# Linear attention, MLP and Sinkhorn mixture of experts on one core: VectorE's queue taken from the scheduler, and eight weight conversions placed at other steps

## The chip, the cores and the metric

One core of a Trainium2 chip. The metric is the time of one run of the program in device microseconds (us); lower is better. The engines are named as in the profile: PE (TensorE, PEld its weight loads), DVE (VectorE), ACT (ScalarE), POOL (GpSimd) and SP (SyncE, which issues the transfers). Each engine works through its own queue, one instruction after the other, in an order fixed when the program is built; waits between engines go through semaphores.

## What is computed

The reference, cut to what matters:

```python
# attention: q, k, v are 4 x 8 x 576 x 64
q_s = softmax(q, axis=-1); k_s = softmax(k, axis=2)
kv  = einsum('bhsd,bhse->bhde', k_s, v)
x   = einsum('bhsd,bhde->bhse', q_s, kv)      # -> 2304 tokens x 512
# MLP: w_in 512 x 2048, w_out 2048 x 512
h = x @ w_in
x = maximum(0.01 * h, h) @ w_out
# experts: 8, each w1 512 x 1024, w2 1024 x 512
P = exp(x @ w_gate - max)
for _ in range(8):                            # Sinkhorn
    P /= P.sum(1) + 1e-9; P /= P.sum(0) + 1e-9; P *= N / E
out = sum over e of P[:, e] * (relu(x @ w1[e]) @ w2[e])
```

Matrix products are made of three matmuls each: both operands are held as a high and a low part, and high x high, high x low and low x high are added up in PSUM.

## The kernel before, in words

The program has three stages that overlap on the engines.

**Attention.** `k_task` (line 251) takes the exponential of one pair of heads of k: DVE finds the maximum (`knm`, L255), ACT the exponential with its sum (L257), PE transposes (`pk`, L265), ACT copies to `ke` (L267), PE multiplies with v (`pkv`), ACT scales into `kv` (L281). `q_task` (line 283) does the softmax of 128 tokens of q in place in `acc`: DVE maximum (`qmx`, L291), POOL subtraction (L293), ACT exponential (L295), DVE sum and reciprocal (`qsm`, L297 to L299), POOL product (L300), PE transpose (`pq`, L305), ACT copy back (L306). `x_task` (line 308) multiplies both (`px`) for one block of 384 tokens and splits the result into its high part (ACT, L331) and low part (DVE, L332) in `xs`. There are six blocks.

**MLP.** 96 steps: four phases of four 128-wide weight units over six blocks. A step `s` has two half-steps: in half-step 2s, `first` makes the hidden group `ph` (12 matmuls) of step s+1 (before step 14) or s+2, and ACT and DVE turn it into `hh` (L205 to L207); in half-step 2s+1, `second` multiplies `hh` of step s into four output groups `y0` to `y3` (12 matmuls). At a block's last unit the four groups are copied to `acc` by ACT (L226, in the first phase) or added to it by DVE (L228); the next block's `y` groups use the same four PSUM banks. The weights of the MLP arrive as 64-bit floats, and `prep_half` (line 138) converts half a unit over four half-steps: ACT absolute value (`ca`, L146); one half-step later three DVE ops (L148, L149, L152); one later the ACT cast of the high part (L156) and two DVE ops (L157, L158); one later a subtraction and an addition (L162, L163), on DVE for the first four units and on POOL for the others, and then the load of another half unit. Three raw buffers hold the loads.

**Experts.** 48 groups `group(i)` (line 571), each of seven parts with Strassen-like sums, and output tiles `e`. Gate and Sinkhorn (`balance`) run at its beginning.

What sets the order: up to the experts all code runs inside `tc.manual_schedule()` (line 74, closed at line 772 by `front.close()`), where each engine's queue is the order in which the source calls its instructions. The half-steps are a hand-written plan: `at(t, task)` starts a task in half-step t, and each `yield` of the task hands over to the next half-step. Behind line 772 the scheduler orders every queue by its own rules.

Of the kernel before, what the change touches and what calls it, by code (L numbers as in the profile page):

```python
# [22 lines left out]
def kernel(  # L23
# [47 lines left out]


    front = ExitStack()
    front.enter_context(tc.manual_schedule())
    const = ctx.enter_context(tc.tile_pool(name="const", bufs=1))
    hp_ = ctx.enter_context(tc.tile_pool(name="h", bufs=2))
    sk_p = ctx.enter_context(tc.tile_pool(name="sk", bufs=2))
# [45 lines left out]
    halves = ((0, 0), (1, 0), (0, 1), (2, 0), (1, 1), (3, 0), (2, 1), (3, 1))  # L123
# [526 lines left out]
    def at(t, f, *a):  # L650
        plan.setdefault(t, []).append((f, a))
# [74 lines left out]
    at(26, open_units)  # L726
    H2 = 2 * SP

    for t, (f, half) in zip((26, 28, 29, 32, 34, 36, 40, 42), halves):
        at(t, prep_half, PU + f, half)  # L730
    for ph in range(1, NPH - 1):
        for n, (f, half) in enumerate(halves):
# [40 lines left out]
    t = END  # L773
# [47 lines left out]
```

## Time and profile before

| | |
|---|---|
| median of 3 runs | 2020.96 us (2019.91 to 2023.77) |
| the profiled execution | 2021.46 us, its span 2019.6 us |
| busy in the span | PE 1990.9 us, PEld 1825.1, DVE 1300.8, ACT 806.7, POOL 486.5 |
| instructions | 26345 |
| moved by transfers | 138.56 MB, 68 GB/s from and to memory over the span |

The span is cut at times from its start. In a timeline row the first number is the start, the second the time from the first start to the last end of the merged instructions, xN their count, and the bracket the engine's idle time before it with what ended that. A wait belongs to the engine that idles. PEclk is the granted TensorE clock as a share of full speed.

### The profile page before, as it was taken

What the parts mean: (1) busy time and instruction counts of PE and PEld (TensorE: products, weight loads), DVE (VectorE), ACT (ScalarE), POOL (GpSimd) and SP (SyncE); (2) the same over time, 40 slices, a digit from 0 to 9 for tenths busy, and PEclk for the clock granted to TensorE, in tenths of its full rate; (3) what the DMA queues carried; (4) which work ended last, traced back from release to release, by engine and by line L of the source; (5) the groups of instructions that cost most, each with busy time, mean ns of one, the idle gap of its engine ahead of it and who ended that gap; (6) DMA issues with size and microseconds to landing.
All of it is one profiled execution on the core that took longest, in us unless ns stands there. A gap on an engine that the chain in (4) does not pass through costs nothing.

```text
span 2019.6 us, 26345 instructions
## 1 busy us (share of the span) xinstructions
PE 1990.9 (99%) x10323; PEld 1825.1 (90%) x10323; DVE 1300.8 (64%) x1953; ACT 806.7 (40%) x1367; POOL 486.5 (24%) x476
## 2 busy tenths in 40 slices
PE   7999999999999999999999999999999999999998
PEld 6999999999889999989999999999999999999997
DVE  7766435445786666666766666666686666666663
ACT  6654323234443333333444333334344333333331
POOL 3124222300223223122122231231322322313220
PEclk7999999999999999999999999999999999999999
DMA  6502111100212212212132122121212221211210
GB/s 221 175 12 81 45 43 42 53 1 1 85 43 84 84 42 84 70 56 84 42 115 84 43 84 73 54 84 48 78 68 89 84 82 44 84 55 72 84 42 32
DMA packets 65453, 138.56 MB, mean 69 GB/s; under 512 B 4656, under 2 KB 4656, under 8 KB 65328
## 3 DMA queue, kind: packets, MB, share of 16 engines
q1 hardware_dynamic: 65328, 136.87, 19.6%
q8 instruction: 81, 1.33, 0.3%
q14 instruction: 44, 0.36, 0.1%
HBM read 132.14 MB, written 4.72 MB: 68 GB/s over the span
## 4 chain that ended last, share of the span: by engine, by line
PE 73%; DVE 1%; ACT 0%; issue 0%; ACTq 0%; DVEq 0%
PE e L189 38%; PE pa L189 10%; PE pc L189 10%; PE pd L189 10%; PE pb L189 5%; DVE wa L458 0%; PE y L189 0%; DVE xs L565 0%; ACT wa L457 0%; DVE pm L399 0%; DVE cs L400 0%; PE pcs L189 0%; PE pt L189 0%; PE pg L189 0%; DVE rs L398 0%; DVE rs L396 0%
## 5 line engine op out<-in xcount | busy, mean ns | idle before, releaser
L189 PE MATMUL e<-wb_t,xs 128*128 128x512 f32 x3456 | 803.4, 390 | 0.0
L189 PEld LDWEIGHTS e<-wb_t,xs 128*128 128x128 f32 x3456 | 647.0, 188 | 131.2
L464 POOL TENSOR_TENSOR s<-pair 128x256 f32<-128x256 f32 x96 | 72.5, 755 | 1186.1 <-DMA pair<-in_w 719.3
L558 DVE SCALAR_TENSOR_TENSOR acc<-e,pm,acc 128x512 f32<-128x512 f32 x264 | 193.0, 743 | 99.5 <-PE e L189 98.3
L189 PE MATMUL pa<-xs,wa 128*128 128x384 f32 x1152 | 234.2, 337 | 0.0
L565 DVE SCALAR_TENSOR_TENSOR xs<-c,xs 128x384 fp32r<-128x384 f32 (+1 forms) x192 | 185.2, 983 | 70.9 <-ACT xs L564 70.9
L189 PE MATMUL pc<-xs,wa 128*128 128x384 f32 x1152 | 230.8, 334 | 0.0
L189 PE MATMUL pd<-xs,wa 128*128 128x384 f32 x1152 | 230.6, 334 | 0.0
L564 ACT ACTIVATE xs<-c 128x768 fp32r<-128x768 f32 x192 | 126.8, 682 | 231.8 <-PE e L189 211.1
L189 PEld LDWEIGHTS pa<-xs,wa 128*128 128x128 f32 x1152 | 204.6, 188 | 7.2
L189 PEld LDWEIGHTS pc<-xs,wa 128*128 128x128 f32 x1152 | 202.4, 188 | 0.2 <-issue 0.2
L189 PEld LDWEIGHTS pd<-xs,wa 128*128 128x128 f32 x1152 | 202.4, 188 | 0.1
L207 DVE TENSOR_TENSOR hh<-g,hh 128x384 fp32r<-128x384 f32 x96 | 58.4, 609 | 197.8 <-ACT g L206 197.8
L458 DVE TENSOR_TENSOR wa<-s,wa 128x768 fp32r<-128x768 f32 x96 | 91.8, 957 | 106.1 <-ACT wa L457 106.0
L457 ACT CAST wa<-s 128x768 fp32r<-128x768 f32 x96 | 80.2, 836 | 170.8 <-POOL s L467 150.2
L580 DVE TENSOR_TENSOR c<-c 128x384 f32<-128x384 f32 x96 | 53.9, 561 | 133.4 <-ACT c L600 133.4
L590 ACT COPY c<-pa 128x384 f32<-128x384 f32 x96 | 46.1, 480 | 198.9 <-PE pa L189 193.5
L458 DVE TENSOR_TENSOR wa<-pair,wa 128x1024 fp32r<-128x1024 f32 x96 | 120.2, 1252 | 5.2 <-ACT wa L457 5.1
L205 ACT ACTIVATE hh<-ph 128x384 fp32r<-128x384 f32 x96 | 47.3, 492 | 184.1 <-PE y L189 170.6
L458 DVE TENSOR_TENSOR wb_t<-pair,wb_t 128x1024 fp32r<-128x1024 f32 x96 | 114.1, 1223 | 7.0 <-PE y L189 3.2
L189 PE MATMUL y<-hh,wa 128*128 128x384 f32 x576 | 112.4, 344 | 4.2 <-ACT acc L226 3.6
L467 POOL TENSOR_TENSOR s<-pair,s 128x256 f32<-128x256 f32 x96 | 113.8, 1185 | 7.5
(117 smaller groups left out, 2528.7 us busy)
## 6 DMA issues: line engine op xcount, KB each, us to landing
pair<-in_w SPq DMA_DIRECT2D x192, 512.0 KB, 5.1
raw<-in_wm SPq DMA_DIRECT2D x32, 512.0 KB, 3.8
v<-in_vt SPq DMA_DIRECT2D x16, 320.0 KB, 5.8
k<-in_kt SPq DMA_DIRECT2D x16, 288.0 KB, 5.6
out<-acc SPq DMA_DIRECT2D x18, 256.0 KB, 2.0
acc<-in_q SPq DMA_DIRECT2D x5, 768.0 KB, 7.6
acc<-in_q SPq DMA_DIRECT2D x3, 256.0 KB, 6.3
wg_t<-in_wg SPq DMA_DIRECT2D x1, 16.0 KB, 3.5
```

What stands on the lines that cost most here:

```text
L189: nc.tensor.matmul(o, a, b, start=start, stop=stop, **more)
L205: nc.scalar.activation(hh[:, 0, :], p, AF.Prelu, alpha=0.01)
L207: nc.vector.tensor_tensor(hh[:, 1, :], g, r32(hh[:, 0, :]), op=ALU.subtract)
L457: nc.scalar.copy(hi, a)
L458: return lambda: nc.vector.tensor_tensor(lo, a, r32(hi), op=ALU.subtract)
L464: nc.gpsimd.tensor_tensor(s[:, 0], a21, a22, op=ALU.add)
L467: nc.gpsimd.tensor_tensor(s[:, 2], a12, s[:, 1], op=ALU.subtract)
L558: nc.vector.scalar_tensor_tensor(a, y, scale, a, op0=ALU.mult, op1=ALU.add)
L564: nc.scalar.activation(o[:, 0], p, AF.Relu)
L565: nc.vector.scalar_tensor_tensor(o[:, 1], p, 0.0, r32(o[:, 0]), op0=ALU.max, op1=ALU.subtract)
L580: add = lambda o, x, y: nc.vector.tensor_tensor(o, x, y, op=ALU.add)
L590: nc.scalar.copy(c1, bk[0])
```

## The change

```diff
     front = ExitStack()
-    front.enter_context(tc.manual_schedule())
+    E_ = mybir.EngineType
+    front.enter_context(
+        tc.manual_schedule(engines={E_.PE, E_.Activation, E_.Pool, E_.SP})
+    )
...
-    for t, (f, half) in zip((26, 28, 29, 32, 34, 36, 40, 42), halves):
+    for t, (f, half) in zip((26, 28, 32, 34, 36, 41, 43, 45), halves):
         at(t, prep_half, PU + f, half)
```

The first part takes DVE out of the manual order: up to the experts its queue is now what the scheduler makes of it, while PE, ACT, POOL and SP keep the order of the source. The second gives six of the eight conversions of the second phase's units other half-steps: none is left one half-step behind another, and the last one begins at 45 instead of 42.

The instructions are the same ones, 1953 on DVE in both programs. The queues of PE, POOL and SP hold them in the same order as before. On ACT the conversions between `hh16` and `hh25` have moved, and two casts of the second pair of expert weights stand three instructions earlier, ahead of `hh87`. On DVE most of the queue up to the experts is rearranged. Three places follow; the line numbers of the change are three higher, the number behind a name's last underscore is the buffer's, and `ca4_1` is unit 4, half 1.

**DVE in the startup**, behind the first conversion; `knm1_0` is the maximum of the first heads of k of batch 1, `qmx` and `qsm` belong to tiles of q, `ksm` to sums of k. Before:

```order
L163 TENSOR_TENSOR wa_84<-ca0_0_156,raw0_0_123 128x512
L255 TENSOR_REDUCE knm1_0_225<-k1_0_158 128x1
L291 TENSOR_REDUCE qmx2_228<-acc0_77 128x8
L268 TENSOR_SCALAR ksm0_2_166<-ksm0_2_166 128x1
L269 RECIPROCAL ksm0_2_166<-ksm0_2_166 128x1
L291 TENSOR_REDUCE qmx3_258<-acc1_78 128x8
L268 TENSOR_SCALAR ksm0_3_186<-ksm0_3_186 128x1
L269 RECIPROCAL ksm0_3_186<-ksm0_3_186 128x1
L297 TENSOR_REDUCE qsm1_189<-acc0_77 128x8
```

In the change:

```order
L166 TENSOR_TENSOR wa_84<-ca0_0_156,raw0_0_123 128x512
L294 TENSOR_REDUCE qmx2_228<-acc0_77 128x8
L271 TENSOR_SCALAR ksm0_2_166<-ksm0_2_166 128x1
L271 TENSOR_SCALAR ksm0_3_186<-ksm0_3_186 128x1
L272 RECIPROCAL ksm0_2_166<-ksm0_2_166 128x1
L272 RECIPROCAL ksm0_3_186<-ksm0_3_186 128x1
L300 TENSOR_REDUCE qsm1_189<-acc0_77 128x8
L301 TENSOR_SCALAR qsm1_189<-qsm1_189 128x8
L302 RECIPROCAL qsm1_189<-qsm1_189 128x8
L294 TENSOR_REDUCE qmx3_258<-acc1_78 128x8
L294 TENSOR_REDUCE qmx4_300<-acc1_78 128x8
L258 TENSOR_REDUCE knm1_0_225<-k1_0_158 128x1
```

`knm1_0` stood right behind the conversion's last op; it now stands behind the sum of q tile 1 (`qsm1`, which reads what ACT's exponential writes) and two more maxima.

**ACT at steps 15 to 17**, where block 3's output is copied to `acc3`. Before:

```order
L205 ACTIVATE hh16_1605<-ph16_1592 128x384
L206 ACTIVATE g16_1606<-ph16_1592 128x384
L146 ACTIVATE ca4_1_1617<-raw4_1_1114 128x512
L156 CAST wb_t_1533<-ca5_0_1572 128x512
L205 ACTIVATE hh17_1650<-ph17_1637 128x384
L206 ACTIVATE g17_1651<-ph17_1637 128x384
L156 CAST wb_t_1533<-ca4_1_1617 128x512
L226 COPY acc3_80<-y0_12_1505 128x384
L226 COPY acc3_80<-y1_12_1506 128x384
L226 COPY acc3_80<-y2_12_1507 128x384
L226 COPY acc3_80<-y3_12_1508 128x384
```

In the change:

```order
L208 ACTIVATE hh16_1605<-ph16_1592 128x384
L209 ACTIVATE g16_1606<-ph16_1592 128x384
L159 CAST wb_t_1533<-ca5_0_1572 128x512
L208 ACTIVATE hh17_1645<-ph17_1632 128x384
L209 ACTIVATE g17_1646<-ph17_1632 128x384
L229 COPY acc3_80<-y0_12_1505 128x384
L229 COPY acc3_80<-y1_12_1506 128x384
L229 COPY acc3_80<-y2_12_1507 128x384
L229 COPY acc3_80<-y3_12_1508 128x384
L149 ACTIVATE ca4_1_1670<-raw4_1_1114 128x512
```

The cast of unit 4's second half stood between `g17` and the four copies; it now comes behind them, after its absolute value.

**DVE at the end of a block in the last phase**: the additions into `acc2`, the split of a summed block (L458, `xs<-acc1`) and `hh85`. Before:

```order
L458 TENSOR_TENSOR xs_83<-acc1_78,xs_83 128x768
L458 TENSOR_TENSOR xs_83<-t1_0_4059,xs_83 128x768
L207 TENSOR_TENSOR hh85_4160<-g85_4161,hh85_4160 128x384
L458 TENSOR_TENSOR xs_83<-acc1_78,xs_83 128x768
L228 TENSOR_TENSOR acc2_79<-y0_80_4043,acc2_79 128x384
L228 TENSOR_TENSOR acc2_79<-y1_80_4044,acc2_79 128x384
L228 TENSOR_TENSOR acc2_79<-y2_80_4045,acc2_79 128x384
L228 TENSOR_TENSOR acc2_79<-y3_80_4046,acc2_79 128x384
L357 TENSOR_TENSOR xs_83<-acc2_79,xs_83 128x768
L207 TENSOR_TENSOR hh86_4198<-g86_4199,hh86_4198 128x384
```

In the change:

```order
L461 TENSOR_TENSOR xs_83<-acc1_78,xs_83 128x768
L461 TENSOR_TENSOR xs_83<-t1_0_4059,xs_83 128x768
L231 TENSOR_TENSOR acc2_79<-y0_80_4043,acc2_79 128x384
L231 TENSOR_TENSOR acc2_79<-y1_80_4044,acc2_79 128x384
L231 TENSOR_TENSOR acc2_79<-y2_80_4045,acc2_79 128x384
L231 TENSOR_TENSOR acc2_79<-y3_80_4046,acc2_79 128x384
L210 TENSOR_TENSOR hh85_4160<-g85_4161,hh85_4160 128x384
L461 TENSOR_TENSOR xs_83<-acc1_78,xs_83 128x768
L360 TENSOR_TENSOR xs_83<-acc2_79,xs_83 128x768
L493 TENSOR_TENSOR acc1_78<-acc1_78,t1_0_4059 128x768
L210 TENSOR_TENSOR hh86_4198<-g86_4199,hh86_4198 128x384
```

The four additions, which free the `y` banks, stood behind `hh85` and a split that waits for ACT; they now stand ahead of both.

## Rows read from the trace of the kernel before

**Rows 1.** The page, busy time of each engine (share of the span, instructions).
```profile
PE 1990.9 (99%) x10323; PEld 1825.1 (90%) x10323; DVE 1300.8 (64%) x1953; ACT 806.7 (40%) x1367; POOL 486.5 (24%) x476
```

**Rows 2.** Stretches: start:end, length, busy PE, PEld, DVE, ACT, POOL, PEclk, DMA share, GB/s.
```profile
0.00:48.65 48.65, 37.33 (x172) 30.45 (x173) 37.59 (x77) 30.79 (x71) 19.26 (x23) 0.72 0.62 217
60.00:67.30 7.30, 5.42 (x25) 5.39 (x26) 5.37 (x9) 3.65 (x8) 0.81 (x1) 0.77 0.33 103
...
570.00:2019.00 1449.00, 1444.57 (x7257) 1308.11 (x7255) 967.68 (x1317) 562.14 (x853) 346.32 (x360) 1.00 0.20 69
```

**Rows 3.** Waits of PE by its line and the releaser: us, times, longest.
```profile
PE pk L265 <- ACT k L257: 6.4, 3, 3.3
PE y L189 <- ACT acc L226: 3.6, 2, 2.6
...
PE ph L189 <- DVE xs L332: 1.9, 1, 1.9
PE y L189 <- DVE acc L228: 1.7, 2, 1.2
...
PE ph L189 <- ACT ke L267: 1.0, 1, 1.0
```

**Rows 4.** DVE in the startup: a stretch, and two lines' durations (ns min/median/max) there.
```profile
20.00:42.26 22.26, 17.91 (x65) 13.63 (x65) 21.54 (x45) 15.73 (x38) 11.06 (x10) 0.54 0.42 147
L149 DVE TENSOR_SCALAR ca<-ca x4: 1146/1147/1149, 9.4 to 55.3; 128x512 uint32<-128x512 uint32 x4
L158 DVE SCALAR_TENSOR_TENSOR raw<-raw x4: 692/1411/1415, 12.6 to 59.9; 128x512 f32<-128x512 uint32 x4
```

**Rows 5.** Timeline, startup: where its splits and the first hidden groups stand.
```profile
18.74 0.63 ACT L295 ACTIVATE acc<-acc 128x512 f32<-128x512 f32 x1 [1.97 <-POOL acc L293]
19.26 0.75 DVE L255 TENSOR_REDUCE knm<-k 128x1 f32<-128x576 f32 x1 [1.45 <-DMA k<-in_kt]
21.62 0.67 DVE L297 TENSOR_REDUCE qsm<-acc 128x8 f32<-128x512 f32 x1
42.26 1.00 DVE L332 TENSOR_TENSOR xs<-px,xs 128x384 fp32r<-128x384 f32 x2
48.65 4.41 PE L189 MATMUL ph<-xs,wa 128*128 128x384 f32 x24
```

**Rows 6.** Timeline, block 1's splits, and what PE does before and behind its wait.
```profile
61.28 1.01 DVE L332 TENSOR_TENSOR xs<-px,xs 128x384 fp32r<-128x384 f32 x2
61.88 1.18 PE L189 MATMUL ph<-xs,wa 128*128 128x384 f32 x5 [1.88 <-DVE xs L332]
64.41 3.19 PE L189 MATMUL y<-hh,wa 128*128 128x384 f32 x12
66.45 0.43 DVE L149 TENSOR_SCALAR ca<-ca 128x512 uint32<-128x512 uint32 x1
...
77.21 2.36 PE L189 MATMUL y<-hh,wa 128*128 128x384 f32 x12
```

**Rows 7.** Timeline, conversions of the second phase: ACT's cast and copies, PE behind them.
```profile
161.78 1.53 DVE L148 TENSOR_SCALAR ca<-ca 128x512 f32<-128x512 f32 x1
165.50 0.62 ACT L156 CAST wb_t<-ca 128x512 fp32r<-128x512 f32 x1 [2.75 <-DVE ca L152]
166.03 1.62 ACT L226 COPY acc<-y 128x384 f32<-128x384 f32 x4
166.55 2.39 PE L189 MATMUL y<-hh,wa 128*128 128x384 f32 x12 [2.62 <-ACT acc L226]
184.64 2.38 PE L189 MATMUL y<-hh,wa 128*128 128x384 f32 x12 [1.01 <-ACT acc L226]
```

**Rows 8.** Timeline, last phase: the additions of two blocks and PE behind them.
```profile
463.36 1.94 DVE L228 TENSOR_TENSOR acc<-y,acc 128x384 f32<-128x384 f32 x4
464.05 2.35 PE L189 MATMUL y<-hh,wb_t 128*128 128x384 f32 x12 [1.15 <-DVE acc L228]
484.01 2.35 PE L189 MATMUL y<-hh,wb_t 128*128 128x384 f32 x12 [0.59 <-DVE acc L228]
```

## The prediction

> **What bounds the kernel now.** I read the busy times first: PE works 1990.9 of 2019.6 us [rows 1], so the whole program runs at PE's pace, and another engine's order counts only where PE waits for it or runs at the low clock. The stretches say where that is [rows 2]. From 570 us on PE idles 4.4 of 1449 us, and that is the end of the span; this is the expert stage, whose queues the change leaves alone. Up to 48.65 us, before the first hidden group, PE is granted 0.72 of full speed and is busy 37.33 us. At 60 us the clock falls once more, to 0.77 over 7.3 us. The list of PE's waits gives the rest [rows 3]: `y` for ACT's copies 3.6 us in two pieces, `ph` for a split (L332) 1.9, `y` for DVE's additions 1.7 in two pieces, `ph` for ACT's `ke` 1.0. The 6.4 us for k's exponentials lie in the startup. These are some 20 us in all, counting lost clock, and the change can reach nearly all of them: PE, POOL and SP keep their order, so what moves is when DVE and ACT deliver.
>
> **The change, part by part.** The sum is made against the profiled execution, 2021.46 us; the median shown, 2020.96, lies 0.5 lower, and 0.2% (4.0 us) is about what a measurement of this kernel can tell from no change.
>
> *Startup, to the first hidden group.* Between 20.00 and 42.26 us DVE is busy 21.54 of 22.26 us [rows 4], and at 42.26 it begins the first split that `ph` of step 0 needs [rows 5]. So its queue sets this stage. The new queue holds the same instructions ahead of that split, but for one maximum more and a few short ones; what can differ is how long they take and whether DVE idles. L149 took 1.15 us in each of its four runs here and 0.43 later [rows 4, 6]; L158 took 1.41 in the middle case and 0.69 at best [rows 4]. The long forms are those with a POOL op running beside them, 0.72 us more each; in the timeline of this stretch six conversion ops have them. I followed the new queue through this stage by hand, row by row, with the durations of the old trace and each op started when its input or the op ahead of it ends. The first maximum of batch 1 (`knm1_0`) comes out about 0.9 us later; the sums of the q tiles come 1 to 2 us earlier, POOL and ACT follow them, the other maxima of k are long done when ACT asks, and three conversion ops are long instead of six (2.2 us). The first split begins at about 39.7, 2.6 us earlier. PE's own chain of transposes at the low clock stands between that and `ph`, so I pass on half: **-1.25 us**. Bounds: -2.6 if all is passed on; +2.9 if four further ops fall beside POOL, ten in all (4 x 0.72), and nothing else improves.
>
> The Trainium skill (SBUF — State Buffer, section Who interferes with whom) puts it harder: the port pair of DVE and GpSimd is an exclusive lock, whichever issues first keeps it for its whole instruction, and a DVE reduction never contends. By that rule alone, a queue that mixes conversions among reductions may come out at either end of those bounds, the upper one included.
>
> *The split at 61.88.* PE waits 1.88 us for block 1's third split, which DVE begins at 61.28, behind a sum and two conversion ops, and which ends only as PE resumes [rows 6]. In the new queue those stand ahead of `hh1`, which waits for PE anyway, and what is left in front is one maximum of k, the end of that conversion and one maximum of q. By the same walk the split comes at 59.1 and PE waits about 0.9 us: **-0.95**, between 0 and -1.88. Behind this wait 12 `y` matmuls take 3.19 us instead of 2.36 [rows 6] at a clock of 0.77 over 7.3 us [rows 2], 1.7 us lost. Of the waits in rows 3, 7 and 8 this alone is followed by a lower clock, and it comes behind a stage at the low one; with half the wait I take the clock as kept: **-1.7**, between 0 and -1.7.
>
> *`ke` at 104.* The 1.0 us are ACT's, late because a maximum of k was late on DVE [rows 3]; the new queue puts these maxima earlier: **-1.0**, between 0 and -1.0.
>
> *Conversions of phase 2.* At 165.50 ACT's cast has waited 2.75 us for DVE, whose L148 took 1.53 us beside POOL; the four copies stand behind the cast, and PE's `y` waits 2.62 us for them [rows 7]. In the new order no cast stands between `g17` and the copies, and the cast ahead has its input long before, since its DVE ops now go ahead of `hh15`. The 1.01 us at 184.64 come from three conversions in a row, each a round from DVE to ACT and back that is longer than PE's step; with DVE's ops moved ahead of the `hh` ops the round is broken. **-3.63**; 0 if the waits only move (a rival).
>
> *Additions in the last phase.* The additions that free the `y` banks begin at 463.36 behind `hh85` and a split, and PE waits 1.15 us, then 0.59 at 484.01 [rows 8]. The new queue puts them first in one place; in the other an op stands between the first and the second, which PE's first three matmuls cover. **-1.74**. The `hh` ops moved back are read two steps later, and a step is 24 matmuls, 4.4 us [rows 5]; without that cover each would cost its 0.56 us. The two casts ahead of `hh87` are costed at nothing under the same cover.
>
> *Moved for nothing.* In phases 2 and 3 between 200 and 420 us many DVE ops change places with PE at work throughout. *New waits.* A queue that is rearranged over 450 us will hold one somewhere; the rows bound it by nothing and by the largest of this kind, 2.62 [rows 7]. I take the middle, **+1.3**.
>
> Sum: -1.25 - 0.95 - 1.7 - 1.0 - 3.63 - 1.74 + 1.3 = -9.0. From 2021.46 that is 2012.5, against the median 2012.0. With the bounds of its own terms the forecast reaches from 2008.5 to about 2016.
>
> **The rivals.**
>
> *Only the later waits go.* The startup keeps its time, since its chain also runs through ACT, POOL and PE at the low clock, and `ph`'s wait at 61.88 stays with its clock. Then -3.63 - 1.74 - 1.0 + 1.3 to 2.6, some 2015.5 to 2017; with a startup at +1 to +2 it ends at 2017 to 2018.5, within 0.2%. For it: PE's first maxima are not earlier, `knm1_0` is later. Against: DVE is the engine that is full there.
>
> *The copies' wait moves.* The new ACT order has the cast of `ca7_1` directly ahead of block 5's copies, as `ca4_1` was ahead of block 3's. If its DVE ops are late by as much, the 2.62 come back and the time is about 2014.5 to 2016. Against: two hidden groups of ACT lie between its absolute value and its cast.
>
> *Slower: DVE and ACT in lock-step at the startup.* DVE takes its queue strictly in order; `knm1_0`, until now waiting only for its load at 19.26, stands behind `qsm1`, which needs the exponential that ACT began at 18.74 for 0.63 us [rows 5]. From 19.37 the sum and two maxima (three reductions at 0.67) put it at 21.4, its two short ops at an estimated 21.8, 2.5 us late, and ACT, PE and the next exponential wait behind it. If that repeats at the five exponentials of q tiles 1 to 5, it is 12.5 us, and with -3.63, -1.74 and -1.0 elsewhere the time is 2027.5, or 2027 against the median. It decides from the third round on: three rounds (7.5) outweigh the 6.4. Against: only `knm1_0` stands so close behind a sum; the next three have a lead of several ops. The Trainium skill (TensorE: Matmul & The Clock Gate, section Architectural detail: the array is 16× 32×32, not 1× 128×128) says that ACT and DVE are strict first-in, first-out queues, which is what this case rests on; DVE's 1.45 us of idle time ahead of `knm`, with other work behind it, agrees.
>
> **How the numbers follow.** Forecast 0.52, only the later waits 0.28 (0.10 of it still faster by over 0.2%), the moved wait 0.10 (faster), lock-step 0.10. Faster than 2016.9: 0.52 + 0.10 + 0.10 = 0.72; within 0.2%: 0.18; slower than 2025: 0.10. The range leaves out the lock-step and the outermost part of the rest: 2008 to 2018.5, about 8 in 10.
>
> **What would show it.** In the profile of the changed kernel: the first `ph` at about 47.4 us; the `ph` wait for L332 under 1.2 us and the clock at 1.00 from there on; no wait of PE for ACT's L229 (L226 before) over 0.5 us between 150 and 210; no wait for L231 (L228 before) at 460 to 490; the expert stage as before, only earlier. I am wrong if `ph` begins later than 48.65, if a wait for the copies stands at another block, or if PE's waits for DVE name a maximum or sum that now stands ahead of a split.

## The result, and the profile after

The change took 2002.95 us (median of 3 runs, 2001.37 to 2004.33) against 2020.96 before: a ratio of 0.9904, 95% interval 0.9885 to 0.9924. That is 18.0 us less; 9.0 were forecast, and the range ended at 2008. The profiled execution of the change took 2004.33 us with a span of 2002.5, 17.1 less than that of before. The page of the change, busy times:

```profile
PE 1982.4 (99%) x10323; PEld 1823.8 (91%) x10323; DVE 1302.3 (65%) x1953; ACT 802.4 (40%) x1367; POOL 476.9 (24%) x476
```

Stretches of the change, columns as in [rows 2]:

```profile
0.00:48.65 48.65, 36.41 (x191) 31.12 (x192) 36.26 (x87) 32.95 (x78) 19.91 (x25) 0.86 0.66 237
60.00:67.30 7.30, 7.30 (x40) 6.47 (x39) 5.70 (x11) 5.25 (x13) 0.00 (x0) 1.00 0.28 104
570.00:2002.00 1432.00, 1428.61 (x7176) 1294.31 (x7174) 954.17 (x1294) 553.36 (x840) 342.18 (x355) 1.00 0.20 69
```

The startup has more of the full clock (0.86 after 0.72 in [rows 2]), the dip at 60 us is gone, and the expert stage is as before: PE idles 3.4 us in 1432. PE's waits in the change (line, releaser: us, times, longest):

```profile
PE pk L268 <- ACT k L260: 7.2, 3, 3.8
PE pkv L192 <- ACT ke L270: 1.6, 2, 1.2
PE y L192 <- ACT acc L229: 1.5, 2, 1.3
```

Of the waits in [rows 3] that for `ph` on a split, that for `ph` on `ke` and that for `y` on DVE's additions no longer show, and that for `y` on the copies fell from 3.6 to 1.5. The wait for k's exponentials grew from 6.4 to 7.2. These waits of PE's matmuls account for some 6 of the 17 us. The rest can be found by following one instruction that each of the 96 steps has: ACT's first activation of the hidden group (`hh<-ph`). Steps 0, 3, 8, 17, 26, 85 and 95, timeline of ACT before:

```profile
51.02 0.49 ACT L205 ACTIVATE hh<-ph 128x384 fp32r<-128x384 f32 x1 [0.51 <-PE ph L189]
...
70.17 0.49 ACT L205 ACTIVATE hh<-ph 128x384 fp32r<-128x384 f32 x1 [1.45 <-PE ph L189]
...
106.29 0.49 ACT L205 ACTIVATE hh<-ph 128x384 fp32r<-128x384 f32 x1 [0.26 <-PE ph L189]
...
161.88 0.49 ACT L205 ACTIVATE hh<-ph 128x384 fp32r<-128x384 f32 x1 [0.56 <-PE y L189]
...
203.86 0.49 ACT L205 ACTIVATE hh<-ph 128x384 fp32r<-128x384 f32 x1 [1.81 <-PE y L189]
...
460.85 0.49 ACT L205 ACTIVATE hh<-ph 128x384 fp32r<-128x384 f32 x1 [1.79 <-PE y L189]
...
511.38 0.49 ACT L205 ACTIVATE hh<-ph 128x384 fp32r<-128x384 f32 x1 [3.99 <-PE y L189]
```

and in the change:

```profile
47.63 0.49 ACT L208 ACTIVATE hh<-ph 128x384 fp32r<-128x384 f32 x1 [0.51 <-PE ph L192]
...
63.34 0.49 ACT L208 ACTIVATE hh<-ph 128x384 fp32r<-128x384 f32 x1 [1.09 <-PE ph L192]
...
98.15 0.49 ACT L208 ACTIVATE hh<-ph 128x384 fp32r<-128x384 f32 x1 [0.54 <-PE ph L192]
...
153.68 0.49 ACT L208 ACTIVATE hh<-ph 128x384 fp32r<-128x384 f32 x1 [2.82 <-PE y L192]
...
193.54 0.49 ACT L208 ACTIVATE hh<-ph 128x384 fp32r<-128x384 f32 x1 [1.33 <-PE y L192]
...
446.00 0.49 ACT L208 ACTIVATE hh<-ph 128x384 fp32r<-128x384 f32 x1 [1.79 <-PE y L192]
...
494.41 0.49 ACT L208 ACTIVATE hh<-ph 128x384 fp32r<-128x384 f32 x1 [3.99 <-PE y L192]
```

The differences of the starts are a ledger, against which the terms of the prediction can be put one by one:

| up to | place | shift so far, us | this stretch | forecast |
|---|---|---|---|---|
| step 0 | startup | -3.39 | -3.39 | -1.25 |
| step 3 | split of block 1 (1.88) and the lower clock behind it (1.57) | -6.83 | -3.44 | -2.65 |
| step 8 | `ke` | -8.14 | -1.31 | -1.0 |
| step 17 | nothing more | -8.20 | -0.06 | 0 |
| step 26 | conversions of phase 2, a new wait among them | -10.32 | -2.12 | -2.33 |
| step 85 | "moved for nothing" | -14.85 | -4.53 | 0 |
| step 95 | additions in the last phase | -16.97 | -2.12 | -1.74 |

(The forecast for the conversions is -3.63 with the +1.3 for new waits.) Two stretches make the error: the startup and, above all, the one from 204 to 461 us.

*Where the 4.53 us lie.* At every fourth step, the end of a block, the step is 0.26 or 0.36 us shorter in the change, fourteen times in that stretch. One of them before, ACT, DVE and PE:

```profile
234.01 0.48 ACT L206 ACTIVATE g<-ph 128x384 f32<-128x384 f32 x1
...
234.52 0.66 DVE L207 TENSOR_TENSOR hh<-g,hh 128x384 fp32r<-128x384 f32 x1 [0.93 <-ACT g L206]
...
235.11 1.94 DVE L228 TENSOR_TENSOR acc<-y,acc 128x384 f32<-128x384 f32 x4
235.77 2.06 PEld L189 LDWEIGHTS y<-hh,wb_t 128*128 128x128 f32 x12 [0.42 <-issue]
235.80 2.35 PE L189 MATMUL y<-hh,wb_t 128*128 128x384 f32 x12
```

and the same block end in the change:

```profile
221.35 2.14 DVE L231 TENSOR_TENSOR acc<-y,acc 128x384 f32<-128x384 f32 x4 [1.15 <-PE y L192]
...
222.94 0.49 ACT L208 ACTIVATE hh<-ph 128x384 fp32r<-128x384 f32 x1 [2.82 <-PE y L192]
...
223.84 0.56 DVE L210 TENSOR_TENSOR hh<-g,hh 128x384 fp32r<-128x384 f32 x1 [0.35 <-ACT g L209]
```

Before, the four additions stood behind `hh`, which waits for ACT's `g`, and ended their first piece just too late: the next `y` group's weight loads idled 0.42 us, put down to "issue", where the profile shows nothing that was waited for. The waits of PE's matmuls, which [rows 3] lists, have no line for it. Those of the weight loads have one, and it is the longest of that list (kernel before):

```profile
PEld y L189 <- issue: 7.9, 17, 1.4
```

Fourteen of the 17, 5.3 us, lie between 205 and 460 us, the other three in the last phase; the list of the change has no such line. In the change the additions go first and start as the `y` groups end.

*The startup.* The first split of block 0 begins at 38.37 us instead of 42.26 [rows 5], the first hidden group at 45.27 instead of 48.65 (timeline of the change):

```profile
20.71 0.74 DVE L258 TENSOR_REDUCE knm<-k 128x1 f32<-128x576 f32 x1
...
38.37 1.01 DVE L335 TENSOR_TENSOR xs<-px,xs 128x384 fp32r<-128x384 f32 x2
...
45.27 4.41 PE L192 MATMUL ph<-xs,wa 128*128 128x384 f32 x24
...
56.05 1.00 DVE L335 TENSOR_TENSOR xs<-px,xs 128x384 fp32r<-128x384 f32 x2
```

The third split of block 1 begins at 56.05, where 59.1 was forecast, and PE does not wait for it.

*The new wait.* At block 5's copies (timeline of the change):

```profile
190.07 0.62 ACT L159 CAST wb_t<-ca 128x512 fp32r<-128x512 f32 x1 [1.39 <-DVE ca L155]
...
190.60 1.61 ACT L229 COPY acc<-y 128x384 f32<-128x384 f32 x4
...
191.12 2.38 PE L192 MATMUL y<-hh,wb_t 128*128 128x384 f32 x12 [1.26 <-ACT acc L229]
```

A cast waits for DVE and the copies stand behind it, as in [rows 7], at the block that the second rival named.

### The profile page after: what moved, and what is told of

The parts are those of the page before. It is cut to its first block, busy times and chain, and to the rows that moved or that the text cites. A ratio compares the mean times of both kernels' runs of the same rounds, so it can differ in the third digit from the quotient of the medians.

```text
span 2002.5 us, 26321 instructions
## 1 busy us (share of the span) xinstructions
PE 1982.4 (99%) x10323; PEld 1823.8 (91%) x10323; DVE 1302.3 (65%) x1953; ACT 802.4 (40%) x1367; POOL 476.9 (24%) x476
## 4 chain that ended last, share of the span: by engine, by line
PE 95%; DVE 3%; ACT 1%; issue 0%; DMA 0%; SPq 0%; ACTq 0%; DVEq 0%
PE e L192 39%; PE pa L192 10%; PE pc L192 10%; PE pd L192 10%; PE y L192 10%; PE ph L192 9%; PE pb L192 5%; PE pkv L192 1%; PE px L192 1%; DVE ca L151 0%; DVE hh L210 0%; PE pg L192 0%; PE pq L308 0%; PE pk L268 0%; DMA raw<-in_wm 0%
## 5 line engine op out<-in xcount | busy, mean ns | idle before, releaser
L192 PE MATMUL pb<-xs,wa 128*128 128x384 f32 x576 | 115.3, 335 | 0.0
```

The costliest lines, as they stand in the source:

```text
L192: nc.tensor.matmul(o, a, b, start=start, stop=stop, **more)
```

## The experiments

The theory after the result: VectorE's order does nearly all of it, by putting what PE waits for ahead of what waits for ACT; the new half-steps do little. Its rivals: the half-steps clear the second phase and what follows; or TensorE's clock, which returned to full at 30 us instead of 42, makes the startup's gain.

### VectorE's order alone

```diff
-    for t, (f, half) in zip((26, 28, 32, 34, 36, 41, 43, 45), halves):
+    for t, (f, half) in zip((26, 28, 29, 32, 34, 36, 40, 42), halves):
```

(against the change)

> VectorE in the scheduler's order, the conversions at their old half-steps. Theory (the order on VectorE does nearly all of it): everything up to 149 us as in the change, step 14's hidden group some 8.2 us earlier than in the kernel before; the thirteen block ends between 200 and 450 us 4.5 us shorter and the last phase 2.1 shorter; only the two waits for ACT's copies in the second phase stay in part, since the cast of unit 4's second half stands ahead of block 3's copies as before, 1 to 3 us. About 2004 to 2007. Rival (the new half-steps are what clears the second phase and the block ends): the copies' waits of 2.62 and 1.01 us stay whole and the block ends keep their 0.36 us each: 2010 to 2012.

Measured: 2002.79 us (4 runs, 2001.98 to 2005.35), ratio to before 0.9911 (0.9896 to 0.9925): the change's time, and a little below what was expected. The wait of 2.62 us at block 3 is gone though the cast stands where it stood: the DVE ops of the conversion ahead of it (`ca5_0`) now go ahead of `hh15`, so its own begin right behind `hh16`, at 150.03 us, and end at 152.62, ahead of the cast at 153.53. Step 18 comes 2.86 us earlier against step 17. The smaller wait, at block 4's copies, has grown from 1.01 to 1.65. The block ends give the same 0.26 and 0.36. The order on VectorE is the whole gain; this rival falls.

### The half-steps alone

```diff
-    for t, (f, half) in zip((26, 28, 29, 32, 34, 36, 40, 42), halves):
+    for t, (f, half) in zip((26, 28, 32, 34, 36, 41, 43, 45), halves):
```

(against the kernel before)

> The conversions at the new half-steps, VectorE in the order of the source. Theory: nothing moves before 149 us; the waits of 2.62 and 1.01 us for ACT's copies go, and a new one comes ahead of block 5's copies, since the last conversion starts at 45 and its cast falls into the half-step of those copies: 1 to 2.6 us. The block ends from 200 us on keep 0.36 us each. About 2017.5 to 2020. Rival (the half-steps do most of the second phase and clear the block ends behind it): 8 us less, 2013.

Measured: 2021.51 us (10 runs), ratio 0.9998 (0.9989 to 1.0007): nothing, 1.5 us above the upper end of the theory. The ledger says why. Step 18 comes 2.89 us earlier, as the cast leaves block 3's copies; then block 5's copies wait behind the last cast, and PE, having waited 1.93 us for them, goes on at a lower clock (0.65 between 200.5 and 204.5 us): steps 26 and 27 give back 3.74. The block ends keep their 0.36.

### The additions ahead of `hh`, in the old order

```diff
     def first(s):
...
-        nc.vector.tensor_tensor(hh[:, 1, :], g, r32(hh[:, 0, :]), op=ALU.subtract)
+        def low():
+            nc.vector.tensor_tensor(hh[:, 1, :], g, r32(hh[:, 0, :]), op=ALU.subtract)
+
+        return low
...
+        def seconds():
+            second(s)
+            for low in lows:
+                low()
```

(against the kernel before; `lows` holds the subtraction only where step s ends a block that is added to `acc`; elsewhere it is issued at once)

> The kernel before, VectorE in the order of the source, with one thing moved: at the end of a block whose groups are added to acc, the four additions stand ahead of the hidden group's subtraction that stood ahead of them. Theory (the additions behind that subtraction, which waits for ACT, hold PE 0.36 us at each of thirteen block ends between 200 and 450 us): 4 to 4.7 us less there, and 0.5 to 2 in the last phase, where two splits still stand ahead: 2014.5 to 2016.5. Rival (the block ends lose their time to conversion ops that run long beside GpSimd): no step between 200 and 450 us changes, 2020.5 to 2021.5.

Measured: 2014.48 us (5 runs, 2012.96 to 2015.89), ratio 0.9966 (0.9953 to 0.9979). In the ledger the fourteen block ends give 4.52 us, each 0.26 or 0.36 and at the same steps as in the change, and the last phase 0.72. A block end of this kernel (timeline):

```profile
231.14 1.94 DVE L231 TENSOR_TENSOR acc<-y,acc 128x384 f32<-128x384 f32 x4
...
233.00 1.19 DVE L208 TENSOR_TENSOR hh<-g,hh 128x384 fp32r<-128x384 f32 x1
233.13 2.28 PE L189 MATMUL y<-hh,wb_t 128*128 128x384 f32 x12
```

`hh` even runs long here, and it costs nothing, since it is read two steps later. So the 4.53 us are this one pair of neighbours in the queue, fourteen times, and one edit of the source gives them without the scheduler. The profiled execution has another 2.0 us in its favour that are not the edit's: 0.43 in the startup and 1.56 at step 3, where this time the clock stayed up.

### The startup by hand, the rest scheduled

```diff
     front.enter_context(
-        tc.manual_schedule(engines={E_.PE, E_.Activation, E_.Pool, E_.SP})
+        tc.manual_schedule()
     )
...
+    front.close()
+    front.enter_context(
+        tc.manual_schedule(engines={E_.PE, E_.Activation, E_.Pool, E_.SP})
+    )
     spare[:] = [(ps_m, "m")]
     first(0)
```

(against the change)

> As the change, but VectorE in the order of the source up to the first hidden group. Theory: the first hidden group begins at 48.65 us within 0.3 as in the kernel before; the wait of 1.88 us for block 1's split and the lower clock behind it go all the same, because the order behind the first hidden group puts the split ahead; the rest as in the change: 3.4 us above it, about 2006.4. Rival (the split's wait and the clock behind it hang on how the startup ends): they stay, 3.4 us more, about 2009.8.

Measured: 2010.07 us (4 runs, 2009.86 to 2011.52), ratio 0.9947 (0.993 to 0.9963): the rival's time, but not its mechanism. The cut is not clean: the scheduler pulled maxima of the later stage forward, two of them ahead of the first split and two more between the third and the fourth, and three loads of k are issued at 25.3, 29.4 and 41.0 us instead of 45.6 to 47.0. Step 0 comes 3.75 us later than before, 7.1 later than in the change, which is the difference of the medians. Then the split's wait and the lower clock are gone all the same (step 2 catches up 2.19, step 3 1.56). So the theory's second half holds and its first was not tested; the next run does that.

### The startup scheduled, the rest by hand

```diff
+    front.close()
+    front.enter_context(tc.manual_schedule())
     spare[:] = [(ps_m, "m")]
     first(0)
```

(against the change, with the old half-steps)

> VectorE in the scheduler's order up to the first hidden group alone, then in the order of the source; the conversions at their old half-steps. Theory (the startup's gain comes from VectorE's order there and is handed on whole): step 0's hidden group 3.4 to 4.3 us earlier than in the kernel before, block 1's split again waited for by some 1.9 us, the waits and block ends behind it as in the kernel before: about 2015.5 to 2018. Rival (the clock that falls at 62 us is an answer to the late startup and falls no more): another 1.6 us less, about 2014.5 to 2016. Second rival (the startup's gain is given back at block 1's split, which then waits for loads): 2020 to 2021.

Measured: 2016.6 us (10 runs, 2013.95 to 2017.67), ratio 0.9974 (0.9964 to 0.9983). Step 0 comes 3.15 us earlier, and all of it is handed on: the wait for block 1's split is back (list of waits),

```profile
PE ph L192 <- DVE xs L335: 1.9, 1, 1.9
```

and 3.89 us are still there at step 95. Of the first rival, the clock behind that wait did stay up, in the profiled execution (stretch 57 to 64 us, the same place 3 us earlier), and 4.75 were gained by step 3:

```profile
57.00:64.00 7.00, 5.27 (x34) 5.20 (x35) 5.56 (x10) 4.09 (x10) 0.66 (x1) 1.00 0.31 96
```

Some 0.9 of them are lost at steps 18 to 20, and again with the clock: behind the 2.62 us for block 3's copies it fell in this profile (0.68 between 164 and 168 us) and not in that of the kernel before (1.00 between 166 and 170), so the 12 `y` matmuls take 3.05 us instead of 2.39 and the next `ph` group 3.17 instead of 2.25.

### Is it TensorE's clock?

```diff
+    FILL = {(0, 1, 0): 5, (1, 0, 0): 5, (1, 1): 3}
...
             m = min(4, SC - c0)
+            for _ in range(FILL.get((b, hp, c0), 0)):
+                mm(pt[:, 0, :], ones, ones, True, True)
...
+        for _ in range(FILL.get((b, hp), 0)):
+            mm(pt, ones, ones, True, True)
```

On the kernel before:

> The kernel before with 13 more matmuls of ones on TensorE in the startup, in three places where it waits for ACT (5, 5 and 3 of 0.43 us), each into a bank that is overwritten next. Theory (VectorE's full queue sets the startup, not TensorE's clock): whether the clock then stays at its upper level or not, the first hidden group begins within 0.6 us of 48.65, and the time is 2020 to 2021.5. Rival (the clock's early return makes the startup's gain): where the clock is at 1.00 from 30 us on, the first hidden group begins at 45 to 46, and the time is 2017 to 2018.

Measured: 2022.88 us (10 runs), ratio 1.0002 (0.9991 to 1.0012): no change, though above the range that was expected. The clock is full from 20 to 28 us where it had been low (this kernel first, then the kernel before),

```profile
20.00:28.00 8.00, 5.69 (x41) 4.65 (x42) 7.76 (x18) 7.55 (x19) 3.28 (x3) 1.00 0.96 335
```

```profile
20.00:28.00 8.00, 6.56 (x28) 5.62 (x29) 7.69 (x20) 6.59 (x16) 3.27 (x3) 0.62 0.93 337
```

and the first hidden group begins at 49.10, 0.45 later. Another 0.95 are lost to a fall of the clock behind block 3's copies, as in the run before (0.57 between 168 and 172 us). The first hidden group does not hang on the clock between 20 and 28 us; what a full clock from 30 us on would do in this queue was not reached, since it fell again.

On the change, with its last conversion at half-step 46:

> The change with the last conversion at 46 and the same 13 matmuls in the startup. Theory: as the last conversion at 46 alone, within 1 us, 2000.5 to 2002.5, since VectorE sets the startup. Rival (the clock): the low stretch between 10 and 30 us is shorter and the first hidden group comes 1 to 2 us earlier still, 1999.5 to 2000.5. Third (the added matmuls stand in the way): 0.5 to 2 us more.

Measured: 2000.70 us (4 runs, 2000.12 to 2003.35), the same as without the matmuls (2000.78, below). The clock is 0.99 from 10 to 20 us, 0.83 without them; the first hidden group begins at 44.24, 0.25 earlier. The added matmuls moved the clock little where it counts; the other profiles differ more in it. Up to the first split, the additions moved in the source's order, and then the startup scheduled with the rest by hand:

```profile
0.00:41.84 41.84, 28.15 (x135) 23.08 (x135) 33.04 (x67) 26.72 (x62) 16.60 (x21) 0.80 0.65 239
0.00:38.60 38.60, 27.24 (x135) 23.05 (x135) 27.59 (x69) 25.45 (x60) 14.75 (x21) 0.82 0.76 283
```

At nearly the same clock, 0.80 and 0.82, the first split stands 3.24 us apart, and DVE's busy time is 33.04 and 27.59. So VectorE's order makes most of the 3.89 us between the kernel before and the change. The clock goes with the rest: in the source's order the first split comes 0.42 us earlier at 0.80 than at 0.68, and in the scheduled order it comes at 38.60, 38.37, 37.43, 37.59 and 37.35 us at a clock of 0.82, 0.82, 0.86, 0.86 and 0.91. Up to 1 us of the startup may be the clock's, from one execution to the next; that it is the cause of these differences was not shown.

### Without GpSimd in the startup

```diff
-        nc.gpsimd.tensor_tensor(qs, qs, mx.to_broadcast([P, H, D]), op=ALU.subtract)
+        if i >= 6:
+            nc.gpsimd.tensor_tensor(qs, qs, mx.to_broadcast([P, H, D]), op=ALU.subtract)
...
-        nc.gpsimd.tensor_tensor(qs, qs, sm.to_broadcast([P, H, D]), op=ALU.mult)
+        if i >= 6:
+            nc.gpsimd.tensor_tensor(qs, qs, sm.to_broadcast([P, H, D]), op=ALU.mult)
```

(against the kernel before)

> The kernel before without GpSimd's two operations on the first six tiles of q (the subtraction of the maximum and the product with the reciprocal of the sum are left out for these 768 tokens, so their softmax is not the reference's); every other queue as before. Theory (VectorE is full in the startup, and eight of its conversion ops up to the first split run 0.72 us longer because GpSimd runs beside them): these ops take 0.43 and 0.69 us, VectorE's busy time up to the first split falls from 33.0 to some 27.5 us, and the first split begins 3.5 to 5.5 us earlier, at 36.8 to 38.8, with step 0's hidden group behind it by as much. Rival (the conversion ops are long for another reason, the transfers of the startup): they stay at 1.15 and 1.41 us, the first split within 1 us of 42.26.

Measured: 2018.05 us (8 runs), ratio 0.9986 (0.9976 to 0.9996). The line that took 1.15 us four times [rows 4], in this kernel's startup:

```profile
L149 DVE TENSOR_SCALAR ca<-ca x3: 427/427/427, 9.7 to 32.9; 128x512 uint32<-128x512 uint32 x3
```

The first split begins at 37.88 us, 4.4 earlier. Busy times up to the first split, before, in the change and in this kernel:

```profile
0.00:42.26 42.26, 31.62 (x135) 25.84 (x135) 33.03 (x66) 26.37 (x62) 16.61 (x21) 0.68 0.66 237
```

```profile
0.00:38.37 38.37, 27.31 (x135) 23.13 (x135) 27.58 (x68) 25.43 (x60) 14.73 (x21) 0.82 0.70 261
```

```profile
0.00:37.88 37.88, 24.97 (x135) 21.25 (x135) 27.27 (x66) 26.37 (x62) 2.06 (x9) 0.86 0.72 264
```

The third of the busy times, DVE's, tells the startup's story. Taking GpSimd away takes 5.8 us off DVE, eight times 0.72. The scheduler's order takes 5.4 off with GpSimd still at work: up to the first split of the change three conversion ops run long, at 1.28, 0.93 and 0.87 us, by 1.3 us in all. Step 0 comes only 2.92 us earlier in this kernel, less than was expected: PE waits 1.91 us for the first split, and behind that wait the clock falls (0.66 between 39 and 44 us; 1.00 between 43 and 48 us in the kernel before), so it takes 7.86 us instead of 6.39 from there to the first hidden group. The wait of 1.88 us at block 1 and the lower clock behind it stay.

### The last conversion one half-step later

```diff
-    for t, (f, half) in zip((26, 28, 32, 34, 36, 41, 43, 45), halves):
+    for t, (f, half) in zip((26, 28, 32, 34, 36, 41, 43, 46), halves):
```

(against the change)

> The change with the last conversion of the second phase at half-step 46 instead of 45. Theory (a conversion whose cast falls into the last half-step of a block stands ahead of that block's copies on ACT and hands them VectorE's delay; half-step 47 is such a one): PE's wait of 1.26 us for ACT's copies of block 5 goes, step 26's hidden group comes 1.5 us earlier against step 17's, and the program is 1.5 us shorter than the change, about 2001.5. Rival (VectorE, slow beside GpSimd, is behind there in any case): the wait stays within 0.3 us, 2003.

Measured: 2000.78 us (4 runs, 2000.37 to 2001.66), ratio to before 0.99 (0.9886 to 0.9915). Step 26 comes 1.51 us earlier against step 17 than in the change, as expected: the copies now go ahead of the cast (timeline),

```profile
187.81 1.64 ACT L229 COPY acc<-y 128x384 f32<-128x384 f32 x4
...
188.94 2.28 PE L192 MATMUL y<-hh,wb_t 128*128 128x384 f32 x12
...
189.30 0.66 ACT L159 CAST wb_t<-ca 128x512 fp32r<-128x512 f32 x1
```

and PE goes on without a wait. It has the lowest median together with the filled one, about 2 us below the change; the intervals against before overlap, so it is the ledger that shows the 1.51.

### ACT's queue scheduled too

```diff
-        tc.manual_schedule(engines={E_.PE, E_.Activation, E_.Pool, E_.SP})
+        tc.manual_schedule(engines={E_.PE, E_.Pool, E_.SP})
```

(against the change, with the last conversion at 46)

> The change with the last conversion at 46 and ACT's queue, too, in the scheduler's order up to the experts. Theory (with VectorE in the scheduler's order what is left of waits for ACT is small: 0.5 us in the second phase, some in the startup): within 2 us of the change with the last conversion at 46, 1999 to 2003. Rival (ACT's order by the source held up the startup, where TensorE waits over 8 us for its exponentials): the first hidden group 2 us or more earlier, under 1999. Third (TensorE waits for an ACT result that the scheduler put late): over 2003, with a wait for ACT of over 1 us that is not there now.

Measured: 2040.88 us (5 runs, 2037.12 to 2043.01), ratio 1.0093 (1.008 to 1.0107): the third outcome, 40 us above the same kernel with ACT's order from the source. PE's waits:

```profile
PE pk L268 <- ACT k L260: 11.7, 2, 8.4
PE y L192 <- ACT acc L229: 7.6, 4, 4.6
PE y L192 <- DVE hh L210: 6.8, 3, 3.2
```

Handing a queue to the scheduler is not good in itself. It pays on VectorE here, and on ACT it costs more than twice what VectorE's gave.

## Why the prediction was wrong

The direction and most of the signs were right: the first hidden group earlier, the clock at 1.00 behind it, no wait for additions at 460 to 490, the expert stage only earlier. Of the copies' waits one over 0.5 us was left, at 191, and it stands at another block, which the prediction had named as a sign of being wrong. The size was half.

**The step that failed** is "Moved for nothing": that between 200 and 420 us DVE ops change places "with PE at work throughout", costed at nothing. PE was not at work throughout: at each of fourteen block ends, twelve of them in that stretch and two shortly behind it, it lost 0.26 or 0.36 us to additions that stood behind `hh`, 4.53 us together, and the run with that pair alone exchanged gives 4.52. I had the mechanism in hand, for the last phase (the third piece of the order shown with the change), and priced it only where the list of PE's waits had a line for it. Before, a step at a block's end takes 4.56 or 4.46 us and the others, up to step 78, 4.20; that comparison was open to me, and so was the list of the weight loads. No choice within the terms could have made up for it: with each at its far bound the sum is -12.55, a time of 2008.4. (The 2016 at the other end leaves out bounds of its own terms, the startup's +2.9 and the 2.62 for new waits among them.)

**The startup's term was mis-sized**: -1.25, measured -3.39, with the mechanism (VectorE's full queue, conversion ops long beside GpSimd) right. Two parts of its working were off. The walk put the first split at 39.7; it came at 38.37 (37.35 to 38.60 in the five profiles of kernels with the scheduled startup), since DVE's busy time up to there fell by 5.4 us. The walk had the number of long ops right, three, but at 0.72 us each, 2.2, where they cost 1.3; and it started each op at the end of the one ahead, while most ops of the new order start some 0.08 us sooner (last section). And half was passed on, for fear of PE's chain of transposes at the low clock. That chain is not at the low clock: the granted clock is 1.00 between 43 and 48 us before, and 1.00 from 38.4 to 45.3 in the change. From the first split to the first hidden group it takes 6.39 us before and 6.90 in the change, which has a wait of 0.58 us for a split there; of 3.89 us only 0.5 were lost.

**The other terms.** The split of block 1 was half-priced: the 1.88 us went whole. The lower clock behind it went (1.57 for 1.7), but the reason given, a shorter wait, is not settled: with the whole wait the clock fell in the profiles of the kernel before, of the half-steps alone, of the filled one and of the one without GpSimd, and it stayed up in those of the exchanged additions and of the scheduled startup. Nor is this wait alone followed by a lower clock, as it seemed from one profile: behind the 2.62 us for block 3's copies the clock fell in the scheduled startup and in the filled kernel, and in the change it fell behind a wait of 1.30 us at 495.67 (0.72 between 496 and 502 us). What decides it stays open, so a term for it is a chance and not a gain. `ke` gave 1.31 for 1.0, and the last phase 2.12 for 1.74. Of the 2.62 us at block 3, each of the two reasons given is enough alone: step 18 gains 2.86 us by VectorE's order and 2.89 by the half-steps. The conversions with the new waits came out at -2.12 for -2.33: the gain was there, and the new wait came where the second rival put it, at block 5's copies, at 1.53 us in the ledger instead of 2.62.

**The rivals.** "Only the later waits go" fell with the startup. The slower case, VectorE and ACT in lock-step, happened once: `knm1_0` ran at 20.71 instead of 19.26 [rows 5], 1.45 us later where the walk had 0.9 and this rival 2.5, and PE's next group behind it came 1.4 us later than before; by 33 us that was made up. My own objection, that only this maximum stands close behind a sum, decided it. The lock rule of the Trainium skill (SBUF — State Buffer, section Who interferes with whom) agrees with the run without GpSimd: two-input ops return from 1.41 to 0.69 us, and the reductions took 0.67 with and without it. The outcome lies beyond the good end of the bounds: the scheduled order handed on more than the 2.6 us that I took as the most.

## What to carry to other kernels

The waits of the matmuls alone do not show all that TensorE loses: a loss of 0.3 us that comes back at every block stood in the list of the weight loads, put down to nothing that was waited for, and in the period of the steps. Read both before an order is costed at nothing. In a queue that runs strictly in order, work that frees a buffer for the bottleneck belongs ahead of work that waits for another engine and is read much later. Where an engine's share of a stage is near 100%, what shortens its ops (here keeping them from running beside GpSimd) is handed on in good part: of 5.4 us off DVE 3.4 reached the first hidden group, of 5.8 us in the run without GpSimd 2.9. Which engines' orders to give to the scheduler is found by trying.

## What was not expected of the hardware

Back to back on VectorE, an op that reads the result of the one ahead starts later than one that doesn't. The sum of a q tile takes 0.67 us; in the run without GpSimd, in the source's order, its successor needs it and starts 0.71 us after it, while in the change a conversion's op stands next and starts 0.59 after (timelines of the two):

```profile
31.46 0.67 DVE L298 TENSOR_REDUCE qsm<-acc 128x8 f32<-128x512 f32 x1
32.17 0.17 DVE L299 TENSOR_SCALAR qsm<-qsm 128x8 f32<-128x8 f32 x1
```

```profile
31.54 0.68 DVE L300 TENSOR_REDUCE qsm<-acc 128x8 f32<-128x512 f32 x1
32.13 1.28 DVE L151 TENSOR_SCALAR ca<-ca 128x512 f32<-128x512 f32 x1
```

These are no chance pair. Up to the first split of the kernel before, all 29 ops that read the result of the op right ahead of them start 34 or 35 ns behind its end, and the 34 others that follow one another closely start 74 to 84 ns ahead of it. In the change three such readers are left. So interleaving two chains of dependent ops, as the scheduler does all through the startup, saves about 0.1 us at each place even on an engine that hardly idles. That it is the dependence was not tried by itself.
